# Chunk 3's transposes and scores among the MLP blocks, two pieces of w_in loaded ahead of it, more blocks split

## Chip, cores, metric

One core of a Trainium2 chip. The metric is device time in microseconds (us) of one execution, the median of several. A profiled execution counts from the first instruction, so its span is shorter than the time: for the kernel before, 211.6 against 213.3 in its trace. All positions below are us from the span's start.

## The reference

```python
# linear attention with decay, batch 4, heads 8, sequence 768, head dim 64
intra = (q_b @ k_b.T * Dmask) @ v_b               # inside a block of the sequence
inter = (q_b * lam_pow) @ kv_state                # from the blocks before it
kv_state = lam_block * kv_state + (k_b * rev_pow).T @ v_b
x = (intra + inter) -> (3072, 512)
out = gelu(x @ w_in) @ w_out                      # 512 -> 2048 -> 512, fp32 in and out
```

## The kernel before

It works in bf16 on chunks of 128 positions. Chunk n is batch n % 4 and sequence step n // 4; four chunks of one step form a group of 512 tokens, which goes through the MLP together. Group 0 has chunks 0 to 3, group 1 has 4 to 7. The order on every engine is fixed by the program: the MLP of a group is a list of blocks, and `visits` puts pieces of attention between them.

```python
    for item in "q0 k1 q1 k2 q2 v1 v2 k3 q3".split():     # k0 and v0 are loaded before
        load(int(item[1]), item[0])
    for lo, hi in [(0, 2), (2, 5), (5, 8)]:               # pieces of w_in, in blocks of 128 columns
        load_w_in(lo, hi)
    load(3, "v")
    for s in range(8, NK2, 4):
        load_w_in(s, s + 4)
    ...                                                   # then w_out, then chunks 4 and on

    def next_state(c):                                    # kv(n) = next_state and take_state
        ...                                               # PE: kv_ps = k_dec.T @ v
        if c.so == 0:
            nc.vector.tensor_mul(new, kv_ps, lam_blk)
        else:
            nc.vector.tensor_add(tmp, kv_ps, states[c.b])     # one input in PSUM (matmul outputs), one in SBUF
            nc.vector.tensor_mul(new, tmp, lam_blk)           # two SBUF inputs

    # mlp_blocks(g): a block makes 128 of the 2048 hidden columns for the group's tokens. The first
    # `split` blocks take three chunks (384 columns); the remainders, 128 columns of the last chunk,
    # four blocks in one instruction group, follow directly behind them.
        split = {0: 8, 1: 4}.get(g, 0)
        blocks = [mm1(kf) for kf in range(NK2)]
        for i, kf in enumerate(range(0, split, 4)):
            blocks.insert(split + i, mm1(kf, T - C, 4))

    outputs(live[2])
    transposes(live[3])
    keep_warm(3)                                          # fillers: matmuls on a tile of zeros
    scores(live[3])
    keep_warm(4)
    for n in range(M):
        decay_k(live[n], nc.vector)                       # k_dec of chunks 0 to 3
    make_lam_blk()

    def first_requests():                                 # GpSimd's part at the end of group 0
        for n in (2 * M, 2 * M + 1):
            request(n)                                    # q_hat on GpSimd, k and q transposed by DMA
        for n in range(M, 2 * M):
            decay_k(live[n], nc.gpsimd)                   # k_dec of chunks 4 to 7
        prefetch(2 * M + 3)                               # loads of chunks 10 and 11
        for n in (2 * M, 2 * M + 1):
            decay_k(live[n], nc.gpsimd)

    visits = {
        (0, 7): [lambda: outputs(live[3])],
        (0, 10): [lambda: kv(0, 1)],
        (0, 13): [lambda: kv(2, 3)],
        ...
        (1, 0): [lambda: scores(live[7])],
        (1, 2): [lambda: outputs(live[7])],
        (1, 5): [lambda: kv(4, 5)],
        (1, 7): [lambda: kv(6, 7)],
    }
```

## Time and profile before

| | before |
|---|---|
| time, median of 3 (lowest, highest) | 213.17 (213.10, 213.54) |
| span of the profiled run | 211.6 |
| PE busy | 203.1 of it |
| first MLP matmul of group 0 | 17.21 |
| second piece of w_in lands | 18.90 |
| first w_out matmul of group 0 | 33.01 |
| first w_out matmul of group 1 | 68.53 |

In the profile PE is the tensor engine, DVE the vector engine, ACT ScalarE, POOL GpSimd and SP SyncE. PE is full nearly everywhere, so the two w_out marks cut the time into three: the front (to 33.01), the stretch from mark to mark (35.52; w_out of group 0 and w_in of group 1, called group 1 below), and the rest (143.0). The lines behind the table are in the prediction.

### The profile page before, as it was taken

To read this page: it belongs to the slowest core of one execution; us is meant where nothing else is said; L and a number is where in the kernel's file an instruction comes from. 1 tells how busy PE (TensorE), PEld (TensorE's weight loads), DVE (VectorE), ACT (ScalarE), POOL (GpSimd) and SP (SyncE) were. 2 spreads that over 40 slices of the span, in tenths; PEclk is the share of its full clock that TensorE was granted. 3 is DMA by queue.
4 is the path that set the end of the run, shared out by engine and by line. 5 is a ranking of instruction groups with operands and counts; after the bars stand their busy time and mean duration, and the time that the engine had idled before them with its cause. 6 is when DMAs were issued, how large, how long until landed. Compare 5 with 4: busy or idle time off the path is not lost.

```text
span 211.6 us, 3545 instructions
## 1 busy us (share of the span) xinstructions
PE 203.1 (96%) x1447; PEld 104.8 (50%) x1472; DVE 76.9 (36%) x122; ACT 87.2 (41%) x153; POOL 103.0 (49%) x118
## 2 busy tenths in 40 slices
PE   7899999999999999999999999999999999999994
PEld 2445744556644455444465444455444464444442
DVE  4768130175393136840414942244542240000000
ACT  5763662326646211566211465311465311566121
POOL 7994533891997956949695295761000000000000
PEclk9999999999999999999999999999999999999999
DMA  8999999999999799999999989999400012100112
GB/s 89 135 160 193 206 207 187 155 210 150 181 86 117 82 163 105 146 129 174 99 145 123 156 154 128 114 173 106 150 0 0 3 50 99 50 3 0 50 50 99
DMA packets 100799, 24.48 MB, mean 116 GB/s; under 512 B 92976, under 2 KB 97840, under 8 KB 100784
## 3 DMA queue, kind: packets, MB, share of 16 engines
q0 software_dynamic: 78592, 13.51, 89.1%
q1 hardware_dynamic: 22192, 10.76, 26.6%
q8 instruction: 11, 0.18, 0.4%
q14 instruction: 4, 0.03, 0.1%
HBM read 27.27 MB, written 6.29 MB: 159 GB/s over the span
## 4 chain that ended last, share of the span: by engine, by line
PE 86%; POOL 5%; DMA 4%; DVE 3%; issue 1%; ACT 0%; POOLq 0%
PE o_ps L275 37%; PE h_ps L263 37%; DMA w_in_t<-in_moe_w_in_dram 4%; PE o_ps L230 3%; PE sc_ps L197 3%; PE o_ps L224 2%; PE kv_ps L209 2%; POOL k_t L66 2%; PE o_ps L289 2%; POOL q_t L66 2%; DVE state L217 1%; DVE tmp L216 1%; PE t_ps L176 1%; POOL v_t L66 1%; POOL w_in_t L90 0%
## 5 line engine op out<-in xcount | busy, mean ns | idle before, releaser
L263 PE MATMUL h_ps<-x_t,w_in_t 128*128 128x512 bf16 (+2 forms) x421 | 85.7, 355 | 0.9 <-DMA w_in_t<-in_moe_w_in_dram 0.3
L275 PE MATMUL o_ps<-w_out_t,g_t 128*128 128x512 bf16 x356 | 81.1, 379 | 1.4 <-issue 1.1
L265 ACT ACTIVATE g_t<-h_ps 128x512 bf16<-128x512 f32 (+1 forms) x99 | 57.8, 584 | 34.5 <-PE h_ps L263 33.4
L263 PEld LDWEIGHTS <-w_in_t 128*128 128x128 bf16 x432 | 39.5, 98 | 41.9 <-DMA w_in_t<-in_moe_w_in_dram 0.7
L275 PEld LDWEIGHTS <-g_t 128*128 128x128 bf16 x368 | 35.0, 98 | 40.8
L201 DVE TENSOR_TENSOR sc_m<-sc_ps,dmask 128x512 bf16<-128x512 f32 x48 | 30.0, 683 | 40.4 <-PE sc_ps L197 40.4
L280 ACT COPY o_sb<-o_ps 128x512 f32<-128x512 f32 x23 | 13.5, 586 | 73.2 <-PE o_ps L275 69.7
L189 POOL TENSOR_TENSOR q_hat<-q_t,lam_p 128x512 bf16<-128x512 bf16 x16 | 16.9, 1058 | 28.5 <-issue 15.4
L66 POOL DMA_DIRECT2D k_t<-in_k_dram x24 | 22.0, 918 | 5.4 <-DMA w_in_t<-in_moe_w_in_dram 2.9
L66 POOL DMA_DIRECT2D q_t<-in_q_dram x24 | 21.6, 898 | 3.5 <-DMA w_out_t<-in_moe_w_out_dram 3.4
L66 POOL DMA_DIRECT2D v_t<-in_v_dram x23 | 20.8, 907 | 3.3 <-DMA w_out_t<-in_moe_w_out_dram 1.6
L169 POOL TENSOR_TENSOR k_dec<-k_t,lam_m 128x512 bf16<-128x512 bf16 x16 | 16.8, 1077 | 0.0
L236 DVE CAST x_t<-o_ps 128x512 bf16<-128x512 f32 x16 | 9.9, 684 | 18.1 <-PE o_ps L230 18.1
L216 DVE TENSOR_TENSOR tmp<-kv_ps,state 128x512 f32<-128x512 f32 x16 | 11.0, 685 | 12.4 <-PE kv_ps L209 12.4
L217 DVE TENSOR_TENSOR state<-tmp,lam_blk 128x512 bf16<-128x512 f32 x16 | 12.9, 804 | 0.6
L324 PE MATMUL idle_ps<-idle 128*128 128x512 bf16 x30 | 10.3, 452 | 1.2 <-DVE idle L105 1.2
L182 DVE TENSOR_TENSOR qT<-t_ps,lam_q 128x512 bf16<-128x512 bf16 x8 | 5.5, 690 | 14.6 <-PE t_ps L176 14.4
L197 PE MATMUL sc_ps<-qT,kT 64*128 64x128 bf16 x192 | 8.2, 217 | 1.0 <-DVE qT L182 0.4
L197 PEld LDWEIGHTS <-kT 64*128 64x128 bf16 x192 | 5.7, 94 | 6.6 <-issue 4.4
L230 PE MATMUL o_ps<-sc_m,v_t 128*64 128x128 bf16 x192 | 7.9, 222 | 0.2
L230 PEld LDWEIGHTS <-v_t 128*64 128x64 bf16 x192 | 5.8, 109 | 2.8 <-issue 1.6
L181 ACT COPY kT<-t_ps 128x512 bf16<-128x512 bf16 x8 | 4.7, 586 | 4.5 <-PE t_ps L176 4.5
(41 smaller groups left out, 70.6 us busy)
## 6 DMA issues: line engine op xcount, KB each, us to landing
out_dram<-o_sb SPq DMA_DIRECT2D x23, 256.0 KB, 2.2
k_t<-in_k_dram POOLq DMA_DIRECT2D x24, 128.0 KB, 4.7
q_t<-in_q_dram POOLq DMA_DIRECT2D x24, 128.0 KB, 5.4
v_t<-in_v_dram POOLq DMA_DIRECT2D x23, 128.0 KB, 6.6
w_out_t<-in_moe_w_out_dram POOLq DMA_DIRECT2D x4, 512.0 KB, 16.4
w_in_t<-in_moe_w_in_dram POOLq DMA_DIRECT2D x2, 512.0 KB, 11.1
w_in_t<-in_moe_w_in_dram POOLq DMA_DIRECT2D x2, 384.0 KB, 8.1
v_f<-in_v_dram SPq DMA_DIRECT2D x1, 256.0 KB, 3.6
```

The costliest lines, as they stand in the source:

```text
L66: nc.gpsimd.dma_start(raw[n, name], chunk_of(name, n))
L169: eng.tensor_mul(c.k_dec, c.k, lam_m[:, :, None].to_broadcast((128, H, D)))
L189: nc.gpsimd.tensor_mul(q_hat, c.q, lam_p[:, :, None].to_broadcast((128, H, D)))
L197: nc.tensor.matmul(sc_ps[hi][:, hp, :], c.kT[p, hp, :], c.qT[p, hp, :], start=True, stop=True)
L201: nc.vector.tensor_mul(c.sc_m[:, :, hi, :], sc_ps[hi], dmask_r[:, :, hi, :])
L216: nc.vector.tensor_add(tmp, kv_ps, states[c.b])
L217: nc.vector.tensor_mul(new, tmp, lam_blk)
L230: nc.tensor.matmul(c.o_ps[hi * D:(hi + 1) * D, hp, :], c.v[:, 2 * hp + hi, :], c.sc_m[:, hp, hi, :], start=(c.so == 0 and hp == 0), stop=T ...
L263: nc.tensor.matmul(h_ps[:, f, :], w, x_t[:, ki, lo:hi], start=(ki == 0 and f == 0), stop=(ki == NK1 - 1), skip_group_check=True)
L265: nc.scalar.activation(g_t[:, kf:kf + n_kf, lo:hi], h_ps, ACT.Gelu)
L275: nc.tensor.matmul(om[io], g_t[:, kf, io * C:(io + 1) * C], w_out_t[:, kf, :], start=(kf == 0), stop=(kf == NK2 - 1))
L280: nc.scalar.copy(o_sb, om[io])
```

## The change

Its intent: start the MLP before chunk 3 is ready. Two pieces of w_in go ahead of chunk 3's k and q; chunk 3's transposes and scores move between MLP blocks; more blocks go without the last chunk (10 in group 0, 8 in group 1), and the visits of group 1 move back by a block or so. Cut from the diff: chunk 3's transposes take their PSUM banks under another tag, and the last instruction group of remainders holds two blocks instead of four, as 10 is no multiple of 4.

```diff
-    for item in "q0 k1 q1 k2 q2 v1 v2 k3 q3".split():
+    for item in "q0 k1 q1 k2 q2 v1 v2".split():
...
-    for lo, hi in [(0, 2), (2, 5), (5, 8)]:
-        load_w_in(lo, hi)
-    load(3, "v")
-    for s in range(8, NK2, 4):
-        load_w_in(s, s + 4)
+    for piece in [(0, 2), (2, 5), "k", (5, 8), "q", (8, 10), "v", (10, 13), (13, 16)]:
+        ...                                  # a letter loads that of chunk 3
...
-        split = {0: 8, 1: 4}.get(g, 0)
+        split = {0: 10, 1: 8}.get(g, 0)
...
-    transposes(live[3])
-    keep_warm(3)
-    scores(live[3])
     keep_warm(4)
-    for n in range(M):
+    for n in range(M - 1):
         decay_k(live[n], nc.vector)
...
-        (0, 7): [lambda: outputs(live[3])],
-        (0, 10): [lambda: kv(0, 1)],
-        (0, 13): [lambda: kv(2, 3)],
+        (0, 5): [lambda: kv(0)],
+        (0, 8): [lambda: transposes(live[3])],
+        (0, 9): [lambda: scores(live[3]), lambda: decay_k(live[3], nc.vector)],
+        (0, 10): [lambda: kv(1), lambda: outputs(live[3]), lambda: kv(2)],
+        (0, 15): [lambda: kv(3)],
...
-        (1, 0): [lambda: scores(live[7])],
-        (1, 2): [lambda: outputs(live[7])],
-        (1, 5): [lambda: kv(4, 5)],
-        (1, 7): [lambda: kv(6, 7)],
+        (1, 1): [lambda: scores(live[7])],
+        (1, 4): [lambda: outputs(live[7])],
+        (1, 6): [lambda: kv(4, 5)],
+        (1, 8): [lambda: kv(6, 7)],
...                                           # other visits: one place later, for the one block more
-        a0, a1, b, st = {1: (10, 22, 27, 31), ...
+        a0, a1, b, st = {1: (12, 23, 28, 32), ...
```

More of the change, by code (lines that the diff above doesn't have):

```diff
@@ L94, in load_w_out @@
         nc.gpsimd.dma_start(w_out_t[:, s * f:(s + 1) * f, :], w_out_r[:, s * f:(s + 1) * f, :])
-    for lo, hi in [(0, 2), (2, 5), (5, 8)]:
-        load_w_in(lo, hi)
-    load(3, "v")
-    for s in range(8, NK2, 4):
-        load_w_in(s, s + 4)
+    for piece in [(0, 2), (2, 5), "k", (5, 8), "q", (8, 10), "v", (10, 13), (13, 16)]:
+        if piece in ("k", "q", "v"):
+            load(3, piece)
+        else:
+            load_w_in(*piece)
     for s in range(NS):
@@ L171, in transposes @@
     def transposes(c, between=lambda: None):
-        t_ps = [bank([128, HP, C], BF16, "m" if c.so == 0 else "sc", "t_ps") for _ in range(2)]
+        t_ps = [bank([128, HP, C], BF16, "m" if c.n < 3 else "sc", "t_ps") for _ in range(2)]
         for dst, src in zip(t_ps, (c.k, c.q)):
@@ L299, in mlp_blocks @@
         for i, kf in enumerate(range(0, split, 4)):
-            blocks.insert(split + i, mm1(kf, T - C, 4))
+            blocks.insert(split + i, mm1(kf, T - C, min(4, split - kf)))
         if g == 0:
@@ L393 @@
     visits = {
-        (0, 7): [lambda: outputs(live[3])],
-        (0, 10): [lambda: kv(0, 1)],
-        (0, 13): [lambda: kv(2, 3)],
-        (0, 26): [lambda: transposes(live[4])],
-        (0, 28): [lambda: transposes(live[5])],
-        (0, 29): [lambda: pair_a(4)],
-        (0, 30): [lambda: transposes(live[6])],
-        (0, 31): [lambda: first_requests()],
-        (0, 32): [lambda: inter(live[4]), lambda: inter(live[5]), lambda: intra(live[4]), lambda: intra(live[5]),
-                  lambda: scores(live[6])],
-        (0, 33): [lambda: transposes(live[7]), lambda: outputs(live[6])],
-        (1, 0): [lambda: scores(live[7])],
-        (1, 2): [lambda: outputs(live[7])],
-        (1, 5): [lambda: kv(4, 5)],
-        (1, 7): [lambda: kv(6, 7)],
+        (0, 5): [lambda: kv(0)],
[3 more added lines that the diff above has]
+        (0, 15): [lambda: kv(3)],
+        (0, 27): [lambda: transposes(live[4])],
+        (0, 29): [lambda: transposes(live[5])],
+        (0, 30): [lambda: pair_a(4)],
+        (0, 31): [lambda: transposes(live[6])],
+        (0, 32): [lambda: first_requests()],
+        (0, 33): [lambda: inter(live[4]), lambda: inter(live[5]), lambda: intra(live[4]), lambda: intra(live[5]),
+                  lambda: scores(live[6])],
+        (0, 34): [lambda: transposes(live[7]), lambda: outputs(live[6])],
+        (1, 1): [lambda: scores(live[7])],
+        (1, 4): [lambda: outputs(live[7])],
+        (1, 6): [lambda: kv(4, 5)],
+        (1, 8): [lambda: kv(6, 7)],
     }
@@ L434 @@
         n = (g + 1) * M
-        a0, a1, b, st = {1: (10, 22, 27, 31), 2: (6, 19, 25, 30)}.get(g, (5, 14, 21, 28))
+        a0, a1, b, st = {1: (12, 23, 28, 32), 2: (6, 19, 25, 30)}.get(g, (5, 14, 21, 28))
         if g == 1:
```

## The prediction

> **What bounds the kernel now.** I read the busy shares and the 40 slices first, to see where the tensor engine is not full.
>
> ```profile
> PE 203.1 (96%) x1447; PEld 104.8 (50%) x1472; DVE 76.9 (36%) x122; ACT 87.2 (41%) x153; POOL 103.0 (49%) x118
> ...
> PE   7899999999999999999999999999999999999994
> ...
> PEclk9999999999999999999999999999999999999999
> DMA  8999999999999799999999989999400012100112
> ```
>
> PE is busy in every slice but the first two and the last, at full clock; the DMA engines are full from the start to about 40 us. So the end moves with two sums alone: PE's own work, and its waits. Waits sit in the start-up. The matmul list by time shows them (start, duration, engine, line, tile, count, in brackets the idle time and its cause):
>
> ```profile
> 13.94 0.73 PE L230 MATMUL o_ps<-sc_m,v_t 128*64 128x128 bf16 x8
> 14.60 0.40 PE L176 MATMUL t_ps<-ident,k_t 128*128 128x128 bf16 x4
> 14.83 0.39 PE L176 MATMUL t_ps<-ident,q_t 128*128 128x128 bf16 x4
> 15.06 0.81 PE L324 MATMUL idle_ps<-idle 128*128 128x512 bf16 x2
> 16.00 0.40 PE L197 MATMUL sc_ps<-qT,kT 64*128 64x128 bf16 x8
> 16.34 1.04 PE L324 MATMUL idle_ps<-idle 128*128 128x512 bf16 x4
> 17.21 1.46 PE L263 MATMUL h_ps<-x_t,w_in_t 128*128 128x384 bf16 x8
> 18.95 3.42 PE L263 MATMUL h_ps<-x_t,w_in_t 128*128 128x384 bf16 x20 [0.28 <-DMA w_in_t<-in_moe_w_in_dram]
> ```
>
> Chunk 3's transposes and scores hold PE from 14.60 to 16.34, much of it filler on the idle tile. The MLP starts at 17.21, does the two blocks of the first w_in piece, and waits until 18.95 for the second. That piece is what the start depends on: the chain of waits runs GpSimd load after load, then the w_in transfer, then PE at 18.95. The vector engine's list for chunk 3 gives the latency of its preparation, and the wait list of the MLP its one other wait:
>
> ```profile
> 15.26 0.69 DVE L182 TENSOR_TENSOR qT<-t_ps,lam_q 128x512 bf16<-128x512 bf16 x1 [1.03 <-PE t_ps L176]
> 16.42 1.29 DVE L201 TENSOR_TENSOR sc_m<-sc_ps,dmask 128x512 bf16<-128x512 f32 x2 [0.47 <-PE sc_ps L197]
> ...
> 61.44 0.68 DVE L216 TENSOR_TENSOR tmp<-kv_ps,state 128x512 f32<-128x512 f32 x1
> ...
> 62.17 0.38 PE L197 MATMUL sc_ps<-qT,kT 64*128 64x128 bf16 x7 [0.30 <-DVE tmp L216]
> ```
>
> From the first transpose (14.60) to the first score (16.00) is 1.40 us; from there to the end of both masked score tiles (17.71) is 1.71 us. In group 1, PE waits for the state update of chunk 7 to free a score bank: scores stop after 61.66 and resume at 62.17, against a usual step of 0.056, so 0.45 us.
>
> **What the Trainium skill says.** "TensorE: Matmul & The Clock Gate", section "Wait — 56ns, not 53.3ns?", gives columns / 2.4 + about 2.5 ns per warm matmul: 215.7 ns for 512, 55.6 for 128. The trace agrees: start to start, the medians are 215, 163 (384 columns) and 55 ns. The 379 in the group table is a pipelined latency, not a cost. Splitting 512 columns into 384 and 128 thus costs about 3 ns per matmul. The same page, "What's actually happening", has the clock halve after an idle window of about 3.4 us; all waits here are far shorter, and the granted clock is full in all 40 slices, so removing three fillers costs no clock. "DMA: Bandwidth & Descriptors", section "Latency and other measured facts", says DMA engines 7 and 15 are usually slower on this path; the profile does not name engines, but most 512 B packets of the first w_in piece are done by 15.0 us and the last near 16.4, so I work with measured landing times, which follow the slowest.
>
> **The change, part by part.**
>
> *Loads.* All go through GpSimd and one backlog. These lines are the issues, then the landing times (last column, us after issue) of w_in blocks 0-1, 2-4 and 5-7:
>
> ```profile
> 8.79 0.93 POOL L66 DMA_DIRECT2D k_t<-in_k_dram  x1
> 9.66 0.94 POOL L66 DMA_DIRECT2D q_t<-in_q_dram  x1
> 10.52 2.31 POOL L90 DMA_DIRECT2D w_in_t<-in_moe_w_in_dram  x3
> ...
> w_in_t<-in_moe_w_in_dram POOLq DMA_DIRECT2D x1, 256.0 KB, 6.0
> ...
> w_in_t<-in_moe_w_in_dram POOLq DMA_DIRECT2D x1, 384.0 KB, 7.6
> ...
> w_in_t<-in_moe_w_in_dram POOLq DMA_DIRECT2D x1, 384.0 KB, 8.5
> ```
>
> The issues start at 10.52, 11.27 and 12.00, so the pieces land at about 16.5, 18.9 and 20.5. k3 and q3 (issue plus 4.5) land at 13.3 and 14.15: one 128 KB load is worth 0.87 us of backlog. Moving both behind the first two pieces makes these land 1.74 earlier: 14.8 and 17.15. Then k3 at 18.0, blocks 5-7 at 19.6 (only q3 was taken from before them: 20.5 - 0.87), q3 at 20.5, blocks 8-9 at about 21.75, v3 at 22.6, the rest of w_in as before at 26.4. The total is the same, so w_out and later chunks land as before.
>
> *Start of the MLP.* After chunk 2's outputs (14.60) come four fillers, 4 x 0.216 = 0.86: the MLP starts at 15.46 instead of 17.21, 1.75 earlier. Two blocks of 384 columns are 8 x 0.163 = 1.30: 16.77. Wait for the second piece until 17.2; three blocks (1.96) to 19.15; one state product (4 x 0.056 = 0.22) to 19.38; wait for blocks 5-7 until 19.65. Before, block 5 began at 18.95 + 1.96 = 20.91. So at this point the kernel is 1.26 ahead, though one state product more is done.
>
> *What is paid back in group 0.* Three blocks: 19.65 to 21.61. Transposes of chunk 3 start there. The latencies above now lie on PE's path: scores can start 1.40 later, at 23.0, while PE has only the transposes (0.46) and one block (0.65) to fill it: about 0.3 idle. Masked scores end 1.71 later, at 24.7, while PE has scores (0.34), one block (0.65) and a state product (0.22): about 0.45 idle. Outputs end at about 25.1. The next thing PE may do is one state product (0.22), then the 128-column remainders of blocks 0 to 9, which need chunk 3's x. ScalarE's copy takes 0.59 plus about 0.1 of semaphore: about 0.5 idle, PE resumes at 25.85. Before, these outputs stood one 384-block ahead of the remainders, which hid that copy. Then 40 remainders x 0.056 = 2.23, six full blocks x 4 x 0.2155 = 5.17, one state product 0.22: the first half of group 0's MLP ends at 33.5, against 33.0 before.
>
> Sum from block 5: before, 12.1 us (20.91 to 33.01); after, 13.85: 0.8 for transposes and scores that moved in, less 0.22 for the state product already done, and 1.25 of three new waits, less 0.1 of old ones. The 1.26 won is spent: +0.5 us.
>
> *Group 1.* Eight split blocks instead of four are 16 more matmul pairs, 0.05 us. The state products of chunks 4-7 now stand behind later blocks, with two 128-column groups (0.9 each) and two full blocks (0.86 each) before the next scores: 3.5 us instead of the 2.6 of three full blocks; between the two state pairs there are two 384-blocks (1.3) instead of two full ones (1.73). PE thus reaches the blocked score matmul about 6.05 us after the first state product, against 5.6 before; the vector engine's chain of four updates needs about 6.0. The 0.45 wait should vanish: about -0.4 net.
>
> Sum: +0.5 - 0.4 = +0.1. Later groups keep their order and their full PE. I lean slightly to the better side, as the landing of blocks 5-7 may have slack in it: 213.1 us.
>
> **Rivals.**
> (1) The earlier start is kept: chunk 3's latencies hide, the 1.75 us lead loses only the 0.8 of moved matmuls, and group 1 adds 0.4: 211.8. For it: fillers and waits before 17.2 really go. Against it: PE order is fixed, and I count only one block inside each latency and none before the remainders.
> (2) Transfers are the bound: the second w_in piece is not sped up by the order, because its slow packets come from the transfer itself; then block 5 starts as before at about 20.5 or later and the waits follow: 214.2. For it: the DMA row is full throughout, and the first pieces drain more slowly (256 KB in 2.4 us) than later ones (512 KB in 2.5). Against it: less data stands before each of the first three pieces.
> (3) Group 1's wait merely moves to another place, as GpSimd's decay of chunks 4-7 ends at 58.1, right where the last state products stand now: +0.5, 213.6. Against it: the products come later after the change.
>
> **Range and chances.** The terms left are the landing of blocks 5-7 (0.4 either way), the three waits (together 0.3), and group 1 (0.3). Together about 0.7, plus 0.2 of spread between runs: 212.3 to 213.9. A 2% change is 4.3 us; the whole start-up prize is 1.75, so both outer chances are one in a hundred.
>
> **What would show it.** In the changed profile: MLP's first matmul near 15.5; block 2 near 17.2 behind a w_in wait; chunk 3's transposes near 21.6; PE waits before its scores (0.3), inside its outputs (0.45) and before the first 128-column matmul (0.5, released by ScalarE's x copy); the first w_out matmul near 33.5; no state-update wait of PE in group 1. If that matmul starts before 32.5, or the x-copy wait is missing, my account of group 0 is wrong; if block 5 starts after 20.3, rival 2 holds.

## The result, and the profile after

213.79 us (213.50 to 214.03, 4 runs) against 213.13 for the kernel before beside it (213.04 to 213.54): ratio 1.0026, 95% interval 1.0008 to 1.0045. A ratio is the mean time of one kernel's fast runs over that of the other's in the same rounds, so not quite the ratio of the medians. Executions over 1.5% slower than the fastest of the same kernel are left out of the means. The change made the kernel slower by a quarter of a percent; the span of the profiled run is longer by only 0.2 us (211.8 against 211.6), and the part on the prediction comes back to the rest. Run again later it gave 1.0032 (1.0004 to 1.0060).

The page of the changed kernel, busy shares and PE's slices:

```profile
PE 203.2 (96%) x1469; PEld 106.1 (50%) x1493; DVE 75.7 (36%) x122; ACT 87.7 (41%) x155; POOL 103.7 (49%) x119
...
PE   7898899999999999999999999999999999999994
```

PE's busy time is the same to 0.1 us. In the slices, the holes of the start have spread from the first two slices to the fourth and fifth. PE's list by time shows where they are now:

```profile
15.51 1.46 PE L264 MATMUL h_ps<-x_t,w_in_t 128*128 128x384 bf16 x8
17.16 2.12 PE L264 MATMUL h_ps<-x_t,w_in_t 128*128 128x384 bf16 x12 [0.18 <-DMA w_in_t<-in_moe_w_in_dram]
19.12 0.39 PE L210 MATMUL kv_ps<-v_t,k_dec 128*128 128x128 bf16 x4
19.89 2.12 PE L264 MATMUL h_ps<-x_t,w_in_t 128*128 128x384 bf16 x12 [0.38 <-DMA w_in_t<-in_moe_w_in_dram]
21.85 0.39 PE L177 MATMUL t_ps<-ident,k_t 128*128 128x128 bf16 x4
...
22.30 0.81 PE L264 MATMUL h_ps<-x_t,w_in_t 128*128 128x384 bf16 x4
23.24 0.40 PE L198 MATMUL sc_ps<-qT,kT 64*128 64x128 bf16 x8
...
24.55 0.24 PE L231 MATMUL o_ps<-sc_m,v_t 128*64 128x128 bf16 x1
25.00 0.38 PE L231 MATMUL o_ps<-sc_m,v_t 128*64 128x128 bf16 x7 [0.21 <-DVE sc_m L202]
25.32 0.40 PE L210 MATMUL kv_ps<-v_t,k_dec 128*128 128x128 bf16 x4
26.06 4.12 PE L264 MATMUL h_ps<-x_t,w_in_t 128*128 128x128 bf16 x47 [0.34 <-ACT x_t L235]
```

The bracket understates a wait, because a matmul's record lasts about 0.16 us longer than the step to the next one (0.22 against 0.055 us for 128 columns). Counted start to start against the usual step, the waits are 0.34 before block 2, 0.55 before block 5, 0.30 before the scores (which the list shows only as 22.30 + 0.65 = 22.95 against 23.24), 0.39 inside the outputs and 0.51 before the remainders. The last three are those of the prediction: the latency of chunk 3's preparation, which the kernel before had beside fillers or other blocks. The changed kernel's first w_out matmul comes at 33.69 instead of 33.01.

Group 1 takes 35.06 instead of 35.52. The vector engine's first state update there, in the kernel before and, second, in the changed one:

```profile
56.54 0.69 DVE L216 TENSOR_TENSOR tmp<-kv_ps,state 128x512 f32<-128x512 f32 x1 [3.21 <-PE kv_ps L209]
57.27 1.39 DVE L217 TENSOR_TENSOR state<-tmp,lam_blk 128x512 bf16<-128x512 f32 x1
```

```profile
57.63 0.69 DVE L217 TENSOR_TENSOR tmp<-kv_ps,state 128x512 f32<-128x512 f32 x1 [2.97 <-PE kv_ps L210]
58.36 0.69 DVE L218 TENSOR_TENSOR state<-tmp,lam_blk 128x512 bf16<-128x512 f32 x1
```

The same instruction takes 1.39 in one and 0.69 in the other. I had not counted on that; it decides how group 1 is to be explained. GpSimd's list of the kernel before shows what ran beside it:

```profile
54.07 4.04 POOL L169 TENSOR_TENSOR k_dec<-k_t,lam_m 128x512 bf16<-128x512 bf16 x4
58.05 0.95 POOL L66 DMA_DIRECT2D k_t<-in_k_dram  x1
```

In the changed kernel k_dec ends at 58.02, and the update starts after it, at 58.36. (k_dec is the keys scaled by the decay; the state products need it.)

### The profile page after: what moved, and what is told of

Read it like the earlier page. It is cut to its first block, busy times and chain, and to the rows that moved or that the text cites. A ratio compares the mean times of both kernels' runs of the same rounds, so it can differ in the third digit from the quotient of the medians.

```text
span 211.8 us, 3591 instructions
## 1 busy us (share of the span) xinstructions
PE 203.2 (96%) x1469; PEld 106.1 (50%) x1493; DVE 75.7 (36%) x122; ACT 87.7 (41%) x155; POOL 103.7 (49%) x119
## 4 chain that ended last, share of the span: by engine, by line
PE 87%; POOL 5%; DMA 4%; issue 1%; DVE 1%; ACT 0%; POOLq 0%
PE h_ps L264 37%; PE o_ps L276 37%; DMA w_in_t<-in_moe_w_in_dram 4%; PE sc_ps L198 3%; PE o_ps L231 3%; PE o_ps L225 2%; PE kv_ps L210 2%; POOL k_t L66 2%; PE o_ps L290 2%; POOL q_t L66 1%; PE t_ps L177 1%; POOL v_t L66 1%; POOL w_in_t L90 1%; DVE sc_m L202 1%; DVE qT L183 0%
## 5 line engine op out<-in xcount | busy, mean ns | idle before, releaser
L266 ACT ACTIVATE g_t<-h_ps 128x512 bf16<-128x512 f32 (+2 forms) x101 | 58.2, 577 | 33.8 <-PE h_ps L264 32.6
L264 PEld LDWEIGHTS <-w_in_t 128*128 128x128 bf16 x456 | 40.5, 98 | 41.2 <-DMA w_in_t<-in_moe_w_in_dram 1.1
L218 DVE TENSOR_TENSOR state<-tmp,lam_blk 128x512 bf16<-128x512 f32 x16 | 11.5, 719 | 0.6
L235 ACT CAST x_t<-o_ps 128x512 bf16<-128x512 f32 x8 | 4.6, 587 | 5.1 <-PE o_ps L231 5.0
```

The lines of the kernel that those rows point to most:

```text
L264: nc.tensor.matmul(h_ps[:, f, :], w, x_t[:, ki, lo:hi], start=(ki == 0 and f == 0), stop=(ki == NK1 - 1), skip_group_check=True)
L266: nc.scalar.activation(g_t[:, kf:kf + n_kf, lo:hi], h_ps, ACT.Gelu)
```

## The experiments

Twelve kernels. All gave correct results. Spread between runs grew to a microsecond and more in some kernels, so where a fraction of a microsecond matters I go by the trace's two marks and name the times beside them. There is one trace for each kernel, and it need not be of a typical run: those of g1_only and after_again are of their fastest run, those of states_early, copy_hidden_decay and states_in_wait of their slowest fast one. The first four shared the runs of the kernel before: 213.33 (213.05 to 213.49, 11 runs).

**states_early.** Is PE's work the bound after block 5, or a latency?

```diff
-        (0, 5): [lambda: kv(0)],
+        (0, 5): [lambda: kv(0, 1, 2)],
-        (0, 10): [lambda: kv(1), lambda: outputs(live[3]), lambda: kv(2)],
+        (0, 10): [lambda: outputs(live[3])],
```

> The changed kernel with the state products of chunks 1 and 2 (0.44 us of PE) moved into the wait for w_in before block 5. My account: after block 5 the path is the latency of chunk 3's preparation and not PE's work, so the waits inside the outputs and before the remainders grow by 0.22 each: no change, first w_out matmul at 33.7, time 213.8. Rival (PE's work is the bound there, and filling an idle stretch pays): 0.44 us faster, first w_out matmul at 33.25, time 213.35.

213.94 (213.28 to 215.22, ratio 1.0030). In the profiled run, the longest of the six, the piece of w_in for blocks 5 to 7 landed at 21.41 instead of 19.84, so the absolute marks are no use. From that landing to the first w_out matmul it took 13.85 us, and in the changed kernel 13.85 as well (19.84 to 33.69). The waits grew as expected; PE's list:

```profile
26.57 0.38 PE L231 MATMUL o_ps<-sc_m,v_t 128*64 128x128 bf16 x7 [0.38 <-DVE sc_m L202]
27.63 4.12 PE L264 MATMUL h_ps<-x_t,w_in_t 128*128 128x128 bf16 x48 [0.67 <-ACT x_t L235]
```

Removing 0.44 us of PE work from this stretch gained nothing: it is bound by latency. It also shows what can move the front from one trace to another: it follows one landing.

**copy_hidden.** Is the wait for ScalarE's x copy real?

```diff
-        split = {0: 10, 1: 8}.get(g, 0)
+        split = {0: 11, 1: 8}.get(g, 0)
```

> The changed kernel with eleven split blocks in group 0, so that block 10 stands between chunk 3's outputs and the remainders that need its x. My account: the 0.5 us wait for ScalarE's x copy goes, the remainders start at about 26.25 instead of 26.06 with 0.65 us more done, the first w_out matmul at 33.2 instead of 33.7: 0.45 us faster than the changed kernel (213.3). Rival (the piece of w_in for block 10, which lands at 24.8, holds it instead, or the wait is no bound): no gain, 213.8.

The front did what I expected: landing to w_out 13.36 instead of 13.85, the mark at 33.10. The time did not: 214.00 over the five fast runs (212.80 to 214.85; a sixth, at 216.29, was slow), ratio 1.0020 (0.9992 to 1.0047). Group 1 took 36.01 instead of 35.06. PE's list there:

```profile
58.61 0.39 PE L210 MATMUL kv_ps<-v_t,k_dec 128*128 128x128 bf16 x4
59.52 0.40 PE L210 MATMUL kv_ps<-v_t,k_dec 128*128 128x128 bf16 x4 [0.53 <-POOL k_dec L170]
```

State products waited 0.24 and 0.69 for k_dec on GpSimd, which in this run began late (q of chunk 8 landed at 52, not 50.7). The last k_dec also took 1.49 us (57.98 to 59.47) where the three before it took 1.04; a state update ran beside it and took 0.81 instead of 0.69, so each took longer beside the other. This is my third rival, which I had set aside.

**g0_only.** The changed kernel with group 1 as before.

```diff
-        split = {0: 10, 1: 8}.get(g, 0)
+        split = {0: 10, 1: 4}.get(g, 0)
...   # the four (1, n) visits and a0, a1, b, st of group 1 as in the kernel before
```

> The changed kernel with group 1 as before: group 0's part of the change alone. My account: the first w_out matmul stays at 33.7 us (0.7 later than before) and group 1's wait of 0.45 us is back, so about 0.7 us slower than before (213.8 to 213.9) and 0.4 slower than the changed kernel of the same rounds. Rival (the parts help each other, group 1's gain is not real): the same as the changed kernel.

213.47 (213.39 to 214.12, ratio 1.0014, 1.0001 to 1.0027). The front is the same (19.79 to 33.64, again 13.85). But group 1 takes 35.01 in the old arrangement, no wait in it, and the first state update takes 0.69 at 57.89, after k_dec has ended at 57.76. My account falls: the later places of the state products are not needed for that gain once group 0 is late.

**g1_only.** The kernel before with group 1's part alone.

```diff
-        split = {0: 8, 1: 4}.get(g, 0)
+        split = {0: 8, 1: 8}.get(g, 0)
...   # the four (1, n) visits and a0, a1, b, st of group 1 as in the changed kernel
```

> The kernel before with group 1's part of the change alone: eight blocks split instead of four, scores, outputs and state products later. My account: the 0.45 us wait of the score matmuls for the fourth state update goes, 16 more matmul pairs cost 0.05, so 0.4 us faster than before (212.7), and group 2 starts 0.4 earlier. Rival (the wait only moves to another place, or is no bound of the end): no change, 213.1.

213.13 (212.46 to 214.11, ratio 0.9993, 0.9972 to 1.0013): in the times no gain that can be told from noise. In the trace, which is of the fastest run, group 1 takes 35.08 and the wait is gone, although the first update still took 1.32. So the edit does what I said when it stands alone, and being late does the same. The two do not add: both remove the same 0.45.

The second call ran beside 213.44 for the kernel before (212.91 to 214.10, 11 runs).

**decay_first.** If k_dec slows the update, move k_dec.

```diff
-        for n in (2 * M, 2 * M + 1):
-            request(n)
         for n in range(M, 2 * M):
             decay_k(live[n], nc.gpsimd)
+        for n in (2 * M, 2 * M + 1):
+            request(n)
         prefetch(2 * M + 3)
```

> The kernel before with one edit: GpSimd scales the keys of chunks 4 to 7 (k_dec) before the two q_hat instead of after them, so about 47 to 51 us instead of 54 to 58. New account of group 1: the vector engine's first state update (two SBUF inputs) took 1.39 us instead of 0.69 because it ran beside k_dec, and that alone made the 0.45 us wait of the scores. Then the update takes 0.69 here, the wait is gone with the state products where they were, and the kernel is 0.4 us faster than before (212.9). Rival (the wait comes from the places of the state products, as I predicted): the wait stays, no change, 213.3.

Both accounts missed: 214.02 (212.83 to 215.50, ratio 1.0033, 0.9999 to 1.0066), group 1 took 36.37. The update took 1.12 us at 57.74 with no k_dec running: GpSimd was issuing DMAs. And a new wait came:

```profile
63.47 0.40 PE L197 MATMUL sc_ps<-qT,kT 64*128 64x128 bf16 x8 [1.18 <-DMA qT<-q_hat]
```

With k_dec out of the way GpSimd issued the loads of chunks 10 and 11 at 54.4 instead of 58.05, into the time of the DMA transposes of chunks 8 and 9. The last of these landed 7.5 us after its issue (55.84 to 63.33), against 3.1 before (54.14 to 57.27). The Trainium skill, "DMA: Bandwidth & Descriptors", section "Issuing engines are not separate DMA queues", says that DMAs of all issuers run on the same 16 engines and interleave; this trace agrees, and shows what it costs.

**copy_hidden_decay.** The edits of copy_hidden and decay_first together.

> copy_hidden with k_dec of chunks 4 to 7 ahead of the q_hat on GpSimd. Account: copy_hidden won 0.5 us in group 0 and lost 0.9 in group 1 to state products that waited for k_dec (0.24 and 0.69). Here those waits go: first w_out matmul at 33.1 to 33.2, the second group's at 68.2, 0.5 us faster than the changed kernel (213.3) and no run far above the others. Rival (the gain in group 0 is lost to something else): 213.8 to 214 again.

214.43 (213.14 to 214.56, ratio 1.0037). The waits for k_dec are gone, the front is 13.36 from the landing again, and group 1 takes 36.55: the same wait for qT, 1.17. The account of copy_hidden's loss holds, the remedy was wrong.

**retimed.** Chunk 3's steps placed by their latencies, with k_dec first and eleven split blocks.

```diff
-        (0, 5): [lambda: kv(0)],
-        (0, 8): [lambda: transposes(live[3])],
-        (0, 9): [lambda: scores(live[3]), lambda: decay_k(live[3], nc.vector)],
-        (0, 10): [lambda: kv(1), lambda: outputs(live[3]), lambda: kv(2)],
+        (0, 2): [lambda: kv(0)],
+        (0, 5): [lambda: kv(1, 2)],
+        (0, 6): [lambda: transposes(live[3])],
+        (0, 8): [lambda: scores(live[3]), lambda: decay_k(live[3], nc.vector)],
+        (0, 10): [lambda: outputs(live[3])],
...   # eleven split blocks in group 0 as in copy_hidden, k_dec first as in decay_first
```

> The changed kernel with chunk 3's steps placed by their latency: state products of chunks 0 to 2 in the two waits for w_in, transposes before block 6, scores before block 8, outputs before block 10, eleven split blocks, k_dec first. Account (latency of the preparation is what holds PE after block 5): waits inside outputs and before the remainders nearly gone, first w_out matmul at 32.5 instead of 33.7, 1.2 us faster than the changed kernel: 212.6. Rival (the transfers of w_in hold it, the latencies only hide them): transposes wait for q3 (20.7) and block 10 for its piece (24.8) so long that w_out starts at 33.3 or later: 213.5.

213.04 (212.55 to 214.50, ratio 0.9998). The front: 12.68 from the landing instead of 13.85, w_out at 31.99. Of the three latency waits none is left; 0.4, counted start to start, remains for the piece of w_in for block 10, the rival's term, in a small size. Group 1 took 35.90, with 0.48 for qT.

**states_in_wait.** The other way round: keep the loads of the kernel before, and put work into the wait that they leave.

```diff
+    make_lam_blk()                      # earlier, behind outputs(live[0])
...
+    for n in range(M - 1):
+        decay_k(live[n], nc.vector)
     transposes(live[3])
-    keep_warm(3)
-    scores(live[3])
-    keep_warm(4)
-    for n in range(M):
-        decay_k(live[n], nc.vector)
-    make_lam_blk()
+    keep_warm(2)
...
+        (0, 0): [lambda: kv(0, 1), lambda: keep_warm(1), lambda: kv(2)],
+        (0, 2): [lambda: scores(live[3]), lambda: decay_k(live[3], nc.vector)],
         (0, 7): [lambda: outputs(live[3])],
-        (0, 10): [lambda: kv(0, 1)],
-        (0, 13): [lambda: kv(2, 3)],
+        (0, 11): [lambda: kv(3)],
...   # group 1 as in the changed kernel, k_dec first as in decay_first
```

> Built on the kernel before, with its order of loads: the state products of chunks 0 to 2 (0.67 us of PE) in place of fillers ahead of the MLP, scores of chunk 3 behind block 1, k_dec first, group 1 as changed. Account: block 2 still starts at 18.95 with the second piece of w_in, what is done before it is free, so w_out starts at 32.25 instead of 33.0, and group 1 loses its 0.45 wait: 1.2 us faster than before, 212.1. Rival (fillers were needed, or the vector engine's k_dec ahead of chunk 3's q delays its scores past the wait): 213 or more.

212.79 (212.19 to 213.59, ratio 0.9969, 0.9945 to 0.9993). The front mark stands at 32.25, as expected. Group 1 took 36.56: PE reached the transposes of chunks 5 and 6 before their q had landed and waited 0.38 and 0.72. In this trace, of the longest of the six runs, that cost more than the whole lead: the second mark is at 68.81, against 68.53 before. The times of the other runs show that they kept some of it.

The third call ran beside 213.53 (212.79 to 214.24, 11 runs).

**after_again.** The changed kernel, unedited.

> The changed kernel again, unedited, on the chip and in the rounds of the three below. All accounts: 0.2 to 0.3% slower than before (213.7 to 214), first w_out matmul within 0.3 us of 33.7 where the piece of w_in for blocks 5 to 7 lands near 19.8.

213.96 (213.45 to 215.22, ratio 1.0032). The piece for blocks 5 to 7 landed at 19.25, w_out began at 33.09: 13.84.

**retimed_plain.** retimed without the edit on GpSimd.

> retimed without the edit on GpSimd: chunk 3's steps placed by their latency, k_dec of chunks 4 to 7 behind both q_hat as in the changed kernel. Account: w_out starts at 32.0 to 32.5, but the state products of group 1 then come at 55.7 to 57.9, before k_dec of chunks 5 to 7 (56.1 to 58.1), so about 0.5 to 0.9 of the front's 1.2 to 1.7 is lost in waits for k_dec: about 0.6 us faster than the changed kernel of the same rounds. Rival (GpSimd is no bound in group 1): all of it is kept, 212.3 or less.

213.53 (212.89 to 213.76, ratio 0.9998), 0.4 faster than the changed kernel of the same rounds by the medians. The front mark is at 32.01, group 1 takes 36.50:

```profile
56.47 0.40 PE L210 MATMUL kv_ps<-v_t,k_dec 128*128 128x128 bf16 x4 [0.56 <-POOL k_dec L170]
...
58.92 0.40 PE L210 MATMUL kv_ps<-v_t,k_dec 128*128 128x128 bf16 x4 [0.53 <-POOL k_dec L170]
```

Of the 1.7 that the front gained over the changed kernel's first trace, group 1 gave 1.4 back, each wait being about 0.7 counted start to start. The last k_dec took 1.49 again beside an update. GpSimd is the second bound.

**retimed_spread.** retimed, with k_dec in GpSimd's idle time and the loads left late.

```diff
-        for n in (2 * M, 2 * M + 1):
-            request(n)
-        for n in range(M, 2 * M):
-            decay_k(live[n], nc.gpsimd)
-        prefetch(2 * M + 3)
-        for n in (2 * M, 2 * M + 1):
-            decay_k(live[n], nc.gpsimd)
+        decays(M, M + 1)                 # decays: decay_k on GpSimd of each
+        request(2 * M)
+        decays(M + 2)
+        request(2 * M + 1)
+        decays(M + 3, 2 * M, 2 * M + 1)
+        prefetch(2 * M + 3)
```

> retimed with k_dec of chunks 4 to 7 put into GpSimd's idle time between the two q_hat and the next loads left behind k_dec of chunks 8 and 9 (about 57 us, not 54). Account: decay_first lost because its earlier loads ran into the DMA transposes of chunk 9, so here scores of chunk 9 wait for no qT, state products for no k_dec: first w_out matmul at 32.0 to 32.5, the second group's 35.1 later, about 1.5 us faster than the changed kernel: 212.1. Rival (loads of chunks 4 to 9 are the bound of group 1 whatever GpSimd does): the second group's start stays at 67.9 or later, 213.

213.01 (212.06 to 214.53, ratio 0.9983, 0.9950 to 1.0017). In the trace everything is as expected: w_out at 32.35, group 1 35.06 with no wait for k_dec or qT, span 210.4. But the runs spread over 2.5 us, so the times alone do not show it to be faster than before. The spread lies inside the span (210.2 to 212.6 over the six runs); its cause is open.

**states_spread.** states_in_wait with that order on GpSimd.

> states_in_wait with the same spread on GpSimd. Account: first w_out matmul at 32.25; transposes of chunks 5 and 6 may wait for their q as they did (0.4 and 0.7 there), the rest of group 1 waits for nothing: second group at 67.4 to 68.4, 1 us faster than before (212.2). Rival (as above): 212.8 as states_in_wait.

212.32 (211.83 to 212.67, all six within 0.84): ratio 0.9948, 0.9927 to 0.9968. This beats both kernels: 0.5% faster than before, and 1.6 us below the changed kernel of the same rounds by the medians. PE's list of its start:

```profile
16.02 0.61 PE L209 MATMUL kv_ps<-v_t,k_dec 128*128 128x128 bf16 x8
...
16.91 1.46 PE L263 MATMUL h_ps<-x_t,w_in_t 128*128 128x384 bf16 x8
18.30 0.40 PE L197 MATMUL sc_ps<-qT,kT 64*128 64x128 bf16 x8
18.74 3.42 PE L263 MATMUL h_ps<-x_t,w_in_t 128*128 128x384 bf16 x20
```

State products and scores fill the stretch to the second piece of w_in (landed 18.69), and the 20 matmuls of blocks 2 to 6 start at once. Its marks are 32.13 and 67.66; from one to the other it still waited 0.46, start to start, for q of chunk 5. The first state update starts at 57.27, as in the kernel before, and takes 0.69 instead of 1.39: GpSimd is done with k_dec at 57.15 here, not at 58.11. So the slow update came from the k_dec beside it.

All marks together. "Landing" is of the piece of w_in for blocks 5 to 7 in the upper part, for blocks 2 to 4 in the lower. In retimed and retimed_spread the last wait of the front is not for that piece but for the one of block 10 (landed 24.29 and 24.65, both 7.70 before w_out); in retimed_plain PE got to block 10 just as its piece had landed (24.21).

| kernel | landing to w_out | w_out, group 0 | group 1 |
|---|---|---|---|
| changed; again | 13.85; 13.84 | 33.69; 33.09 | 35.06; 35.06 |
| g0_only | 13.85 | 33.64 | 35.01 |
| states_early | 13.85 | 35.26 | 35.06 |
| copy_hidden; with decay | 13.36; 13.36 | 33.10; 33.11 | 36.01; 36.55 |
| retimed; plain; spread | 12.68; 12.40; 12.67 | 31.99; 32.01; 32.35 | 35.90; 36.50; 35.06 |
| before | 14.11 | 33.01 | 35.52 |
| g1_only | 14.21 | 32.62 | 35.08 |
| decay_first | 14.11 | 33.48 | 36.37 |
| states_in_wait; spread | 13.44; 13.44 | 32.25; 32.13 | 36.56; 35.53 |

## Why the prediction was right, and where it was not

*Range: right.* 213.79 lies in 212.3 to 213.9, near its upper end, and the change is far below 2%.

*Loads: right within 0.35.* Predicted 14.8, 17.15, 19.6 and 21.75 for the first four pieces; measured 15.11, 17.11, 19.84 and 22.09. The slack that I hoped for in the landing of blocks 5 to 7 and leaned on was not there in this trace; over the nine traces with this order of loads that piece landed between 19.25 and 21.41. (A small misreading: the last packet of the first piece ended at 16.21 in the kernel before, not near 16.4. Nothing rests on it.)

*Start of the MLP and group 0: right.* Predicted 15.46 for the first MLP matmul, 17.2 for block 2, 19.65 for block 5, waits of 0.3, 0.45 and 0.5, and w_out at 33.5. Measured: 15.51, 17.16, 19.89, then 0.30, 0.39 and 0.51, and 33.69. From the landing to w_out I had 33.5 - 19.6 = 13.9, and four traces show 13.84 or 13.85. copy_hidden and states_early confirm what kind of waits they are: hiding the copy gains 0.49, taking away work gains nothing.

*Group 1: right in size in the trace, and one step of its cause wrong.* The step that failed is "the vector engine's chain of four updates needs about 6.0". I took the 1.39 us of the first update for a property of the instruction. In the changed kernel the chain takes 5.2, counted like the 6.0 from the first state product (57.21 to 62.43), because the update no longer runs beside k_dec; in its second trace (after_again, front at 33.09) the update still ran 0.33 us beside it, took 0.88, and the chain 5.5, again with no wait. Two things can take the wait away: later places for the state products, as I predicted (g1_only has its front early, at 32.62, its first update slow, and no wait), and a chain that is no longer slowed (g0_only has the old places, its front late, and no wait). The changed kernel has both, so which of them did it cannot be told apart.

*Rival 3, set aside, holds for anything that does better in front.* "GpSimd's decay of chunks 4-7 ends at 58.1, right where the last state products stand now" was true. My answer, that the products come later, was true too, by 1.09 us (56.12 to 57.21), but 0.68 of that is time that group 0 lost. copy_hidden and retimed_plain, with better fronts, ran into the wait.

*The sum: near for the span, too low for the time.* I wrote +0.1 and then leaned the wrong way, to 213.1. The one pair of traces differs by 0.2 us of span (+0.68 in front, -0.46 in group 1). The spans of the timed runs agree: in the rounds of after_again the changed kernel's mean span is 211.88, the other's 211.67. The times there differ by 0.65 in the mean, so most of the difference lies outside the span, of which my sum knew nothing: time less span is 1.72 to 1.84 us in all 33 runs of the kernel before that list both, and 1.90 to 2.04 in eight of the changed kernel's ten, with 2.35 and 3.02 in the others. Neither part of the change has it alone (1.75 to 1.83 in all runs of g0_only and g1_only). What is longer there no trace shows; it stays open. Open is also whether the kernel before loses its 0.45 us in group 1 in every execution: g1_only gained 0.2 in the times, with an interval that holds both 0 and 0.4.

## What to carry to other kernels

Here an earlier start of the large stage was worth nothing, because it exposed latencies that had stood beside other work. Before moving a dependent chain into a full engine's stream, count what stands between its steps, and put enough between all of them (here the last step had nothing). Where a transfer sets a time that the order cannot move, fill the stretch ahead of it with work from behind it; that gained 0.7 us here (14.11 to 13.44 from the landing) with the loads left as they were. And follow a gain to the next engine: GpSimd, and the DMA that it issues, took back front gains of half a microsecond and more until its own order was changed.

## What the Trainium skill lacked or had wrong

- "GPSIMD Engine Reference", section "Specifications", says that VectorE and GpSimd share SBUF interfaces, with contention for vector instructions with two SBUF inputs. This case agrees, and adds sizes that the page lacks: over all 14 traces, 46 state updates (two SBUF inputs) with GpSimd idle took at most 0.693 us; of 178 with GpSimd busy, 63 took over 0.75 and the longest 1.81. The addition just before it, with one PSUM input, never took more than 0.693 (224 of them). Beside k_dec the lengths are regular: of 22 updates that started while a k_dec ran, 19 ended 0.55 or 0.56 us after that k_dec's end, whenever they had started, and three ended 1.55 after it, each with a q_hat begun behind the k_dec. Issuing DMAs from GpSimd could be enough too (1.12 in decay_first, 1.46 in copy_hidden_decay), which the page does not say; but of 83 updates that had only this beside them, 65 stayed under 0.75, the changed kernel's first among them.
- "DMA: Bandwidth & Descriptors", section "Issuing engines are not separate DMA queues", has the interleaving but no size: a DMA transpose landed 3.1 us after its issue with no loads of chunks 10 and 11 issued beside it, and 7.5 us with them.
- No page that I read tells how much the landing of one load varies between executions of one program order: the first piece of w_in, issued at about 8.8 us in each of nine traces with the changed order of loads, landed between 13.8 and 15.1.
